# Attention of a pair of heads in three bursts, its local softmax in three whole-pair operations, and weight rounding on one engine, in a kernel of attention and two feed-forward stages

## The chip, the core and the metric

One core of a Trainium2 chip runs the whole program. It has five engines with a queue each: TensorE (matmuls, its weight loads on a row of their own), VectorE, ScalarE, GpSimd, and SyncE (SP), which here issues all transfers. An engine takes its instructions strictly in the order of its queue and waits for what they need. The metric is the device time of one execution in microseconds (us), the median of several runs; lower is better.

## What is computed

```python
# q, k, v: (4, 8, 576, 64)
q_d = q.reshape(B, H, Sd, 4, D).mean(axis=3)      # k_d, v_d likewise, Sd = 144
out_d = sm_attn(q_d, k_d, v_d)                    # coarse attention
out_up = np.repeat(out_d, 4, axis=2)
mask = np.abs(pos[:, None] - pos[None, :]) < 4    # local attention: a band of 7
out_local = softmax(where(mask, scale * q @ k.T, -1e9)) @ v
x = out_up + out_local                            # heads side by side: (4, 576, 512)
u = x + (x.T @ U @ V).T                           # U: 576x32, V: 32x576
y = u + relu(u @ w_ch1) @ w_ch2                   # 512 -> 2048 -> 512
h = relu(y @ w_in)                                # 512 -> 1024
out = (h * sigmoid(conv3(h))) @ w_out
```

Both softmaxes subtract the row's maximum and divide by the row's sum plus 1e-9.

## The kernel before

The program goes batch by batch. Everything is written out by hand in one order: lists of small functions, "slots", are run between chunks of big matmuls, and each function appends instructions to the queues of the engines it uses. No scheduler moves them afterwards.

**Stages.** In the opening (up to 69.6 us) the attention of batch 0 runs in 29 slots, with the preparation of the first 18 weight chunks and of U and V merged in (`SE`, `NS`), and `keep_warm` puts idle matmuls on TensorE. Then come four windows, `window_a(b)`: the two matmul layers of batch b over 11 of the 16 blocks of the hidden dimension (`g1_pass`, `g2_pass`; 528 big matmuls of 128x288, three for each product, since a number is held as a rounded high part and the rest, `mm3`). Between their chunks the background `bg` runs: the slots of the attention of batch b+1, and in window 0 also the other 26 chunks of weights, in windows 1 and 2 weights that are prepared and stored again (`spill`). After window 3 the five other blocks and the last two layers follow (`g12`, `g34`). I write window 0, 1, 2 for 69.6 to 187.5, 187.5 to 295.8 and 295.8 to 405.9 us.

**Attention.** A unit is a pair of heads, four pairs a batch. The queries of the local part are cut into ten windows of 64 positions (58 new ones each), six in a first group and four in a second (`LI`). The coarse part has two tiles of 72 rows for each head. So a pair has four items: coarse head 0, coarse head 1, local group 0, local group 1. Each goes through scores (matmuls into an accumulator bank), maximum, exponential, normalisation, transposition, copy of the transposed weights, and the product with the values, each step a slot or two after the one before; the items start one slot apart, the pairs five slots apart (four in the opening). The exponential is one ScalarE instruction for every 64-wide window or coarse tile, with the row's maximum as its bias and the row's sum as a second result (L390 to L392). `d_up` spreads the coarse result over four positions, `add_up` adds both into xT. Behind every second pair x is transposed (`x_step`), split into high and low part (`x_hi`, `x_lo`), multiplied with U (`x_g`), and later with V (`h_mix`).

**Banks and buffers.** There are eight accumulator banks. In the windows the big matmuls rotate over three (`psg`) and all of attention over five (`psb`). In the opening attention uses four of one pool and the three of `psg`, one bank being that of the idle matmuls.

**Weights.** A chunk of float64 weights is loaded (L169), turned into float32 words on ScalarE, VectorE and GpSimd (L125 to L142), and split: a rounded copy `dh`, then the rest on GpSimd (L152). The rounded copy is made on VectorE (L151) in the opening and in window 0, on ScalarE (L149) later.

**Transfers.** SP's queue holds, in the order written, q and k (a pair ahead), v twice (`load_vd` for the coarse, `load_vw` for the local part, the latter into tiles that the old values leave free when their last product is done), weight chunks and stores.

## Time and profile before

| | |
|---|---|
| median of three runs | 814.11 us |
| lowest | 813.95 us |
| profiled execution, its own time | 812.12 us |
| its span | 810.3 us |
| TensorE busy (matmuls) | 780.9 us, 96% |
| VectorE busy | 474.4 us, 59% |
| ScalarE busy | 416.4 us, 51% |
| GpSimd busy | 319.2 us, 39% |

The span is what the engines' rows cover; the execution's own time has a little around it. Busy shares are means over stages with different limits, so they are to be read by stretches. Starts are counted from the beginning of the span. A row of small float32 matmuls counts each twice, since it goes through the array in two passes.

### The profile page before, as it was taken

The page shows a single profiled execution, that of the slowest core. Times are in us where ns is not written, and L with a number is a line of the kernel's source. Part 1 is how long each engine was busy: PE and PEld are TensorE (multiplying, and loading weights), DVE is VectorE, ACT ScalarE, POOL GpSimd, SP SyncE. Part 2 cuts the span into 40 slices and gives each one's busy share as a digit, 9 for nine tenths or more (in the row PEclk, how much of TensorE's full clock was granted, in tenths as well). Part 3 has the DMA queues.
Part 4 walks back from the last instruction along what each step waited for, and adds up shares of the span by engine and source line. Part 5 has one row for each costly group of instructions (what it writes and reads, how often), then busy time and mean ns, then how long its engine had stood idle before and what let it go on. Part 6 is the DMA issues. An engine that isn't in the chain of part 4 may idle for free.

```text
span 810.3 us, 17088 instructions
## 1 busy us (share of the span) xinstructions
PE 780.9 (96%) x6355; PEld 719.6 (89%) x6355; DVE 474.4 (59%) x1042; ACT 416.4 (51%) x1308; POOL 319.2 (39%) x417
## 2 busy tenths in 40 slices
PE   6988997999999999999999999999999999999998
PEld 4667886899888998889999999999998999899986
DVE  6999985856766577875441213564265425752563
ACT  6996986624879769787330112432232323322332
POOL 5975674621566445764300011135123411441133
PEclk9799998999999999999999999999999999999999
DMA  7655544426476788557365262200420033002001
GB/s 203 204 145 186 171 140 148 131 88 224 115 216 208 211 270 276 169 144 217 114 251 206 99 210 97 79 1 23 133 74 1 15 128 99 0 10 69 14 1 65
DMA packets 85454, 104.37 MB, mean 129 GB/s; under 512 B 27876, under 2 KB 64124, under 8 KB 85372
## 3 DMA queue, kind: packets, MB, share of 16 engines
q1 hardware_dynamic: 85372, 103.29, 40.5%
q8 instruction: 50, 0.82, 0.4%
q14 instruction: 32, 0.26, 0.1%
HBM read 71.93 MB, written 31.33 MB: 127 GB/s over the span
## 4 chain that ended last, share of the span: by engine, by line
PE 77%; ACT 8%; DVE 5%; DMA 3%; POOL 3%; issue 2%; SPq 1%; POOLq 0%; ACTq 0%; DVEq 0%
PE psg L694 19%; PE psg L695 19%; PE psg L696 19%; PE pso L694 4%; PE pso L696 4%; PE pso L695 4%; DMA cv<-in_moe_w_ch 3%; ACT A L391 3%; ACT cq L125 2%; PE psb L448 1%; PE psb L465 1%; ACT cq L127 1%; ACT cv L126 1%; DVE cv L137 1%; PE psb L549 1%
## 5 line engine op out<-in xcount | busy, mean ns | idle before, releaser
L694 PE MATMUL psg<-h,w 128*128 128x288 f32 x352 | 108.7, 309 | 0.2 <-DVE h L721 0.2
L694 PE MATMUL psg<-uh,w 128*128 128x288 f32 x352 | 108.3, 308 | 0.5 <-ACT uh L580 0.5
L695 PE MATMUL psg<-ul,w 128*128 128x288 f32 x352 | 104.9, 298 | 0.4 <-DVE ul L585 0.4
L696 PE MATMUL psg<-uh,w 128*128 128x288 f32 x352 | 104.6, 297 | 0.0
L695 PE MATMUL psg<-h,w 128*128 128x288 f32 x352 | 104.6, 297 | 0.0
L696 PE MATMUL psg<-h,w 128*128 128x288 f32 x352 | 104.2, 296 | 0.0
L907 POOL TENSOR_TENSOR gl<-cc,gh 128x512 fp32r<-128x512 f32 x32 | 42.4, 1325 | 138.7 <-ACT gh L906 79.2
L142 POOL TENSOR_TENSOR cv<-cv,cq 128x256 int32<-128x256 int32 (+2 forms) x102 | 75.8, 743 | 12.5 <-ACT uh L580 7.5
L892 DVE SCALAR_TENSOR_TENSOR cc<-hb,cw,cc 128x576 f32<-128x576 f32 x64 | 77.2, 1206 | 1.3
L403 POOL TENSOR_TENSOR A<-A,sm 72x288 f32<-72x288 f32 (+1 forms) x64 | 46.8, 732 | 78.5 <-DVE sm L402 36.0
L125 ACT ACTIVATE cq<-cv,tiny 128x256 f16<-128x256 f32 (+2 forms) x102 | 58.8, 577 | 25.8 <-DMA cv<-in_moe_w_ch 19.9
L694 PEld LDWEIGHTS psg<-uh,w 128*128 128x128 f32 x352 | 66.7, 189 | 3.2 <-ACT uh L580 0.8
L694 PEld LDWEIGHTS psg<-h,w 128*128 128x128 f32 x352 | 66.7, 190 | 2.7 <-issue 1.1
L695 PEld LDWEIGHTS psg<-ul,w 128*128 128x128 f32 x352 | 66.6, 189 | 0.6 <-DVE ul L585 0.6
L695 PEld LDWEIGHTS psg<-h,w 128*128 128x128 f32 x352 | 67.1, 191 | 0.0
L696 PEld LDWEIGHTS psg<-h,w 128*128 128x128 f32 x352 | 66.8, 190 | 0.0
L696 PEld LDWEIGHTS psg<-uh,w 128*128 128x128 f32 x352 | 66.5, 189 | 0.0
L880 ACT ACTIVATE hb<-psg 128x288 f32<-128x288 f32 x64 | 26.2, 411 | 76.9 <-PE psg L696 76.3
L720 ACT ACTIVATE h<-psg 128x288 fp32r<-128x288 f32 x88 | 34.8, 396 | 59.7 <-PE psg L696 59.6
L132 DVE TENSOR_SCALAR cv<-cv 128x256 f32<-128x256 f32 (+2 forms) x102 | 52.0, 510 | 18.6 <-ACT cv L126 18.2
L152 POOL TENSOR_TENSOR cv<-cv 128x256 fp32r<-128x256 f32 x52 | 39.0, 750 | 59.7 <-ACT cv L149 51.9
L721 DVE SCALAR_TENSOR_TENSOR h<-psg,h 128x288 fp32r<-128x288 f32 x88 | 39.5, 450 | 29.3 <-ACT h L720 29.3
(168 smaller groups left out, 2290.3 us busy)
## 6 DMA issues: line engine op xcount, KB each, us to landing
cv<-in_moe_w_ch SPq DMA_DIRECT2D x64, 256.0 KB
ws<-cv SPq DMA_DIRECT2D x52, 256.0 KB
wb<-ws SPq DMA_DIRECT2D x15, 512.0 KB
ypb<-ys SPq DMA_DIRECT2D x40, 144.0 KB
w<-ws SPq DMA_DIRECT2D x11, 512.0 KB
qT<-in_q SPq DMA_DIRECT2D x16, 288.0 KB
kT<-in_k SPq DMA_DIRECT2D x16, 288.0 KB
vd<-in_v SPq DMA_DIRECT2D x16, 288.0 KB
```

The costliest lines, as they stand in the source:

```text
L125: nc.scalar.activation(out=q2[:, :, 1].bitcast(F16), in_=x.bitcast(F32), func=AF.Sign, bias=tiny[0:parts])
L132: nc.vector.tensor_scalar(out=xf, in0=xf, scalar1=2 * W_MIN, scalar2=2 * W_MAX, op0=ALU.max, op1=ALU.min)
L142: nc.gpsimd.tensor_tensor(out=t, in0=t, in1=qt, op=ALU.add)
L152: nc.gpsimd.tensor_tensor(out=dl, in0=tv, in1=dh.bitcast(F32), op=ALU.subtract)
L403: nc.gpsimd.tensor_tensor(out=A, in0=A, in1=sm.unsqueeze(2).to_broadcast(list(A.shape)), op=ALU.mult)
L694: nc.tensor.matmul(out=ps, lhsT=lh, rhs=rh, start=first, stop=False)
L695: nc.tensor.matmul(out=ps, lhsT=lh, rhs=rl, start=False, stop=False)
L696: nc.tensor.matmul(out=ps, lhsT=ll, rhs=rh, start=False, stop=last)
L720: after(lambda: nc.scalar.activation(out=h[:, 0, :], in_=ps, func=AF.Relu), lambda: nc.vector.scalar_tensor_tensor(out=h[:, 1, :], in0=ps, ...
L721: lambda: nc.vector.scalar_tensor_tensor(out=h[:, 1, :], in0=ps, scalar=0.0, in1=h[:, 0, :].bitcast(F32), op0=ALU.max, op1=ALU.subtract))
L892: nc.vector.scalar_tensor_tensor(out=cc, in0=hb[:, i:S + i], scalar=cw[:, i * F2 + f:i * F2 + f + 1], in1=cc, op0=ALU.mult, op1=ALU.add)
L907: nc.gpsimd.tensor_tensor(out=lo, in0=cc[:, c0:c1], in1=hi.bitcast(F32), op=ALU.subtract)
```

## The change

The four items of a pair become one unit with three bursts on TensorE: `scores` (local, then coarse, into four banks), `transposes` (coarse, then local, into three banks) and `av` (coarse, then local, into two banks). The pairs stand six slots apart in the windows (scores at slot n, transposes at n+5, values at n+7) and four in the opening (values at n+6), whose table has 27 slots. The table `FIRST` of hand-set places falls away.

The local softmax is one tile for the pair, 128 rows of ten windows of 64: one maximum (`l_max`), one subtraction on VectorE (`l_sub`), one exponential without bias and without sum (`l_exp`), one row sum on VectorE (`l_sum`), one normalisation on GpSimd. The coarse softmax keeps its four exponentials with bias and sum, and has one scaling and one normalisation a pair. The four matmuls of the coarse values alternate between the two heads. `split` makes the rounded copy on ScalarE everywhere. The transposition of x and the product with U come in three steps of up to 512 columns instead of five of 256; their sum has a bank of its own (`psum_g`), and attention rotates over four banks in the windows. `load_vw` of the next pair stands in the slot of `av`. The buffers of q and k go from three to two.

```diff
-    NS, C0, SE, W0, R0, RC = 18, 2, 29, 7, 1, 0.9
+    NS, C0, SE, W0, R0, RC = 18, 2, 27, 7, 1, 0.9
...
     def split(tv, dh, dl):
-        if hi_act[0]:
-            nc.scalar.activation(out=dh, in_=tv, func=AF.Copy)
-        else:
-            nc.vector.tensor_copy(out=dh, in_=tv)
+        nc.scalar.activation(out=dh, in_=tv, func=AF.Copy)
         nc.gpsimd.tensor_tensor(out=dl, in0=tv, in1=dh.bitcast(F32), op=ALU.subtract)
...
+        if pcount[1] and pcount[0] % 2:
+            return psg.tile([P, 512], F32, tag="g", name="psg")
+        return psb[0].tile([P, 512], F32, tag="b", name="psb", bufs=7 - PG - pcount[1])
...
-        for i in range(n):
-            nc.scalar.activation(out=A[:, i], in_=S_ap[:, i], func=AF.Exp, bias=mx[:, i:i + 1], scale=scale,
-                                 accum_out=sm[:, i:i + 1])
+    def l_sub(b, hp):
+        un = units[b, hp]
+        nc.vector.tensor_tensor(out=un.Al, in0=un.Al, in1=un.mxl.unsqueeze(2).to_broadcast([P, NT, WK]), op=ALU.add)
+    def l_exp(b, hp):
+        un = units[b, hp]
+        nc.scalar.activation(out=un.Al, in_=un.Al, func=AF.Exp)
+    def l_sum(b, hp):
+        un = units[b, hp]
+        un.sml = stat("sml", P, NT)
+        nc.vector.tensor_reduce(out=un.sml, in_=un.Al, axis=AX.X, op=ALU.add)
...
+        for kt in range(2):
+            for h in range(2):
+                nc.tensor.matmul(out=un.pso[h * D:(h + 1) * D, :], lhsT=un.vs[:, h * 2 + kt, :],
+                                 rhs=un.ATd[:, h, kt * G4:(kt + 1) * G4], start=(kt == 0), stop=(kt == 1))
...
+        V, A = (4, 6) if first else (6, 7)
...
+            put(n, 0.96 if first else 6, scores, b, hp)
+            put(n + 1, 0.3, l_mask, b, hp, 0)
+            put(n + 1, 0.4, l_mask, b, hp, 1)
+            put(n + 1, 0.6, d_max, b, hp)
+            put(n + 1, 9, d_exp, b, hp)
+            put(n + 2, 0.4, l_max, b, hp)
+            put(n + 2, 0.5, l_sub, b, hp)
+            put(n + 2, 5, l_exp, b, hp)
+            put(n + 3, 0.2, norm, b, hp, "d")
+            put(n + 3, 3, l_sum, b, hp)
+            put(n + 3, 4, norm, b, hp, "l")
+            put(n + 3, 9, v_sum, b, hp)
+            put(n + 5, 6, transposes, b, hp)
+            put(n + 5, 8, at_copy, b, hp)
+            put(n + A, 4, av, b, hp)
```

How the queue of TensorE changes, in window 1. Before, around the second pair (lines of big matmuls left out; L438 coarse transposes, L426 coarse scores, L448 coarse values, L484 local transposes, L465 local scores, L496 local values; xN is the number of matmuls in a row):

```order
L438 MATMUL psb<-ident,A 72x72 x4
L426 MATMUL psb<-kd,qd 72x144 x4
...
L448 MATMUL psb<-AT,vs 64x144 x2
L484 MATMUL psb<-ident,A 128x128 x3
...
L448 MATMUL psb<-AT,vs 64x144 x2
L484 MATMUL psb<-ident,A 128x128 x2
L465 MATMUL psb<-kT,qT 64x64 x12
...
L496 MATMUL psb<-AT,vw_142 64x61 x2
...
L465 MATMUL psb<-kT,qT 64x64 x8
```

After, around one pair (L452 coarse transposes, L456 local transposes, L433 local scores, L438 coarse scores, L478 coarse values, L486 local values):

```order
L452 MATMUL psb<-ident,Ad 72x72 x8
L456 MATMUL psb<-ident,Al 128x128 x5
...
L433 MATMUL psb<-kT,qT 64x64 x20
L438 MATMUL psb<-kd,qd 72x144 x4
...
L478 MATMUL psb<-ATd,vs 64x144 x4
L486 MATMUL psb<-ATl,vw_142 64x58 x2
L486 MATMUL psb<-ATl,vw_143 64x58 x2
```

What stood in five groups between big matmuls stands in three. Between the scores of a window's first pair and its transposes there are 60 big matmuls, between those of the other pairs at least 54 and the values of the pair before.

The queue of ScalarE in window 0, before (L125 to L127 are the start of a weight chunk, L391 the exponentials, L409 the copies of transposed weights, L454 is `d_up`):

```order
L391 ACTIVATE A,sm<-A,mx 128x64 x6
L125 ACTIVATE cq<-cv,tiny 128x256
L126 ACTIVATE cv<-cv 128x256
L127 ACTIVATE cq<-cv 128x256
...
L391 ACTIVATE A,sm<-A,mx 128x64 x4
L409 ACTIVATE AT<-psb 72x288
L125 ACTIVATE cq<-cv,tiny 128x256
L126 ACTIVATE cv<-cv 128x256
L127 ACTIVATE cq<-cv 128x256
L409 ACTIVATE AT<-psb 72x288
L391 ACTIVATE A,sm<-psb,mx 72x144 x2
```

After (L395 coarse exponentials, L494 `d_up`, L404 the local exponential, L146 the rounded copy, L465 the copies of transposed weights):

```order
L395 ACTIVATE Ad,smd<-psb,mxd 72x144 x4
L494 ACTIVATE up<-psb 128x576
L404 ACTIVATE Al<-Al 128x640
L146 ACTIVATE w<-cv 128x256
L125 ACTIVATE cq<-cv,tiny 128x256
...
L465 ACTIVATE ATd<-psb 72x288 x2
L465 ACTIVATE ATl<-psb 128x128
L465 ACTIVATE ATl<-psb 128x512
```

The ten local exponentials are one, the rounded copies have come in, and the four copies of a pair stand together behind four slots of chunk work instead of one by one between chunks.

## Rows read from the trace of the kernel before

**Rows 1.** Busy time by stretches: opening, windows 0 and 1, big matmuls alone

```profile
0.00:69.60 69.60, 55.28 (x598) 40.36 (x599) 59.73 (x159) 59.49 (x221) 52.78 (x83) 0.93 0.60 167
69.60:187.50 117.90, 110.33 (x1034) 101.21 (x1033) 85.30 (x228) 74.72 (x253) 61.61 (x80) 0.97 0.50 158
187.50:295.80 108.30, 106.90 (x1023) 98.21 (x1022) 73.70 (x194) 83.48 (x281) 54.27 (x73) 1.00 0.65 199
...
420.00:440.00 20.00, 20.00 (x153) 20.00 (x152) 2.74 (x6) 1.19 (x3) 0.00 (x0) 1.00 0.72 283
```

**Rows 2.** Waits of TensorE in the whole span: us in total, times, longest

```profile
PE psb L527 <- ACT AT L409: 5.1, 1, 5.1
...
PE psb L484 <- POOL A L403: 2.2, 1, 2.2
```

**Rows 3.** Busy time by stretches, the middle of the opening, columns as in Rows 1

```profile
40.00:60.00 20.00, 16.30 (x188) 12.22 (x189) 18.96 (x48) 19.78 (x75) 16.01 (x22) 1.00 0.51 141
```

**Rows 4.** Timeline of TensorE, window 0: start us, us, engine, line, operation

```profile
82.74 0.92 PE L465 MATMUL psb<-kT,qT 64*64 64x64 f32 x24
...
85.16 0.30 PE L696 MATMUL psg<-uh,w 128*128 128x288 f32 x1
85.38 0.68 PE L465 MATMUL psb<-kT,qT 64*64 64x64 f32 x16
...
86.23 0.29 PE L695 MATMUL psg<-ul,w 128*128 128x288 f32 x1
...
87.57 0.29 PE L696 MATMUL psg<-uh,w 128*128 128x288 f32 x1
87.70 0.43 PE L438 MATMUL psb<-ident,A 72*72 72x72 f32 x4
...
88.15 0.30 PE L695 MATMUL psg<-ul,w 128*128 128x288 f32 x1
```

**Rows 5.** Timeline of TensorE, window 1: two visits with several kinds

```profile
225.94 0.70 PE L448 MATMUL psb<-AT,vs 72*64 72x144 f32 x4
226.58 0.44 PE L484 MATMUL psb<-ident,A 128*128 128x128 f32 x2
...
229.21 0.91 PE L496 MATMUL psb<-AT,vw 128*64 128x61 f32 x24
230.05 0.68 PE L465 MATMUL psb<-kT,qT 64*64 64x64 f32 x16
230.66 0.40 PE L694 MATMUL psg<-h,w 128*128 128x288 f32 x1
```

**Rows 6.** Timeline of ScalarE, two local exponentials in a row

```profile
116.01 0.34 ACT L391 ACTIVATE A<-A,mx 128x64 f32<-128x64 f32 x1
...
116.34 0.34 ACT L391 ACTIVATE A<-A,mx 128x64 f32<-128x64 f32 x1
```

**Rows 7.** Groups by shape, whole span: busy us, mean ns of one

```profile
L896 ACT ACTIVATE cc<-cc 128x576 f32<-128x576 f32 x32 | 21.8, 681 | 17.0 <-DVE cc L892 16.9
L149 ACT ACTIVATE cv<-cv 128x256 fp32r<-128x256 f32 x52 | 21.3, 409 | 0.0
...
L151 DVE CAST w<-cv 128x256 fp32r<-128x256 f32 x44 | 21.3, 483 | 0.2
L899 DVE TENSOR_TENSOR cc<-cc,hb 128x576 f32<-128x576 f32 x32 | 24.2, 758 | 38.5 <-ACT cc L896 38.5
...
L403 POOL TENSOR_TENSOR A<-A,sm 128x384 f32<-128x384 f32 x16 | 14.6, 910 | 11.7 <-DVE sm L402 6.7 <-DVE mx L379 2.7 <-DMA vw<-in_v 1.8
```

**Rows 8.** Timelines of SP and of ScalarE around the wait in window 0

```profile
117.20 3.63 SPq L343 DMA_DIRECT2D vw<-in_v  x4
...
126.95 0.58 ACT L125 ACTIVATE cq<-cv,tiny 128x256 f16<-128x256 f32 x1 [4.64 <-DMA cv<-in_moe_w_ch]
```

**Rows 9.** Timeline of VectorE in the opening, two casts of one shape

```profile
26.08 0.99 DVE L151 CAST vh<-cv 128x192 fp32r<-128x192 f32 x1
...
29.27 0.25 DVE L151 CAST vh<-cv 128x192 fp32r<-128x192 f32 x1
```

More of the change, by code (lines that the diff above doesn't have):

```diff
@@ L287, in s5 @@
         def s5():
-            ps = psum_b()
+            ps = psg.tile([P, 512], F32, tag="g", name="psg")
             nc.tensor.transpose(out=ps[:, 0:n], in_=x["f"], identity=ident[0:n, 0:n])
@@ L306 @@
         pass
-    BUFS = {"vs": 1, "A": 4, "AT": 2}
+    BUFS = {"Al": 2}
     def tmp(b, shape, tag):
-        if b == 0:
+        if b == 0 and tag in ("vs", "Ad", "ATd"):
             return fa.tile(shape, F32, tag="h1", name=tag, bufs=HB)
-        return at.tile(shape, F32, tag=tag, name=tag, bufs=BUFS[tag])
+        return at.tile(shape, F32, tag=tag, name=tag, bufs=BUFS.get(tag, 1))
     units = {}
@@ L395, in soft_add, with stat @@
-    def soft_add(b, hp, key):
-        sm = units[b, hp].sx[key]
+        a, z = LI[i]
+        n = z - a
+        if i == 0:
+            un.Al = tmp(b, [P, NT, WK], "Al")
+        nc.vector.scalar_tensor_tensor(out=un.Al[:, a:z], in0=un.psl[i][:, 0:n * WK].rearrange("p (t c) -> p t c", t=n),
+                                       scalar=SC, in1=msk.unsqueeze(1).to_broadcast([P, n, WK]), op0=ALU.mult,
+                                       op1=ALU.add)
+    def stat(tag, parts, n):
+        return at.tile([P, n], F32, tag=tag, name=tag, bufs=2)[0:parts]
@@ new lines, in d_exp @@
+    def d_exp(b, hp):
+        un = units[b, hp]
+        un.Ad = tmp(b, [GH, 4, G4], "Ad")
+        un.smd = stat("smd", GH, 4)
+        for i in range(4):
+            nc.scalar.activation(out=un.Ad[:, i], in_=un.psd[i // 2][:, i % 2], func=AF.Exp, bias=un.mxd[:, i:i + 1],
+                                 scale=SCD, accum_out=un.smd[:, i:i + 1])
+    def l_sub(b, hp):
+        un = units[b, hp]
+        nc.vector.tensor_tensor(out=un.Al, in0=un.Al, in1=un.mxl.unsqueeze(2).to_broadcast([P, NT, WK]), op=ALU.add)
@@ L416, in keep_warm, with scores @@
             nc.tensor.matmul(out=warm[:, 0:2 * P], lhsT=one[:, 0:P], rhs=one, start=True, stop=True)
-    def d_scores(b, hp, hh):
-        if hh:
-            return
+    def scores(b, hp):
         un = units[b, hp]
+        un.psl = [psum_b(), psum_b()]
         ps = [psum_b(), psum_b()]
+        for i, (a, z) in enumerate(LI):
+            for j in range(a, z):
+                for hh in range(2):
+                    r = slice(hh * D, (hh + 1) * D)
+                    nc.tensor.matmul(out=un.psl[i][r, (j - a) * WK:(j - a + 1) * WK], lhsT=un.qT[r, WS[j]:WS[j] + WK],
+                                     rhs=un.kT[r, WS[j]:WS[j] + WK], start=True, stop=True)
         for t in range(2):
@@ new lines, in av @@
+    def av(b, hp):
+        un = units[b, hp]
+        un.psx = [psum_b(), psum_b()]
+        un.pso = un.psx[1][:, DO:DO + G4]
+        for kt in range(2):
+            for h in range(2):
+                nc.tensor.matmul(out=un.pso[h * D:(h + 1) * D, :], lhsT=un.vs[:, h * 2 + kt, :],
+                                 rhs=un.ATd[:, h, kt * G4:(kt + 1) * G4], start=(kt == 0), stop=(kt == 1))
+        AT = un.ATl.rearrange("p j (h r) -> p j h r", h=2)
+        for i in (1, 0):
+            a, z = LI[i]
+            for j in range(a, z):
+                c, n, o = Q0[j] - WS[j], Q0[j + 1] - Q0[j], Q0[j] - Q0[a]
+                for hh in range(2):
+                    nc.tensor.matmul(out=un.psx[i][hh * D:(hh + 1) * D, o:o + n], lhsT=vw[j % 2][:, j // 2, hh, :],
+                                     rhs=AT[:, j // 2, hh, c:c + n], start=True, stop=True)
@@ L451, in d_up @@
+    DO = 4 * WK
     def d_up(b, hp):
@@ L507, in x_copy @@
         ps, m, w = xs[step]
-        xf = at.tile([P, 2 * P], F32, tag="xh", name="xf", bufs=3)
+        xf = at.tile([P, 4 * P], F32, tag="xh", name="xf", bufs=2)
         nc.scalar.activation(out=xf[0:m, 0:w], in_=ps[0:m, 0:w], func=AF.Copy)
@@ L531, in x_hi @@
         ps, m, w = xs[step]
-        xh = at.tile([P, 2 * P], F32R, tag="xh", name="xh", bufs=3)
+        xh = at.tile([P, 4 * P], F32R, tag="xh", name="xh", bufs=2)
         nc.scalar.activation(out=xh[0:m, 0:w], in_=ps[0:m, 0:w], func=AF.Copy)
@@ L537, in x_lo @@
         ps, m, w, xh = xs[step]
-        xl = at.tile([P, 2 * P], F32R, tag="xl", name="xl", bufs=2)
+        xl = at.tile([P, 4 * P], F32R, tag="xl", name="xl", bufs=1)
         nc.vector.tensor_tensor(out=xl[0:m, 0:w], in0=ps[0:m, 0:w], in1=xh[0:m, 0:w].bitcast(F32), op=ALU.subtract)
```

214 lines of the change are left out of this document (70 added, 144 removed).

## The prediction

> **What bounds the kernel now.** I read the stages first. [rows 1] are five stretches (columns: length, then busy time and instructions of TensorE's matmuls, its weight loads, VectorE, ScalarE, GpSimd, then granted clock, DMA share, GB/s). TensorE is busy 55.28 us of the first 69.60 us, the opening, in which batch 0's attention and the first weights are prepared, and 106.90 of 108.30 us in window 1, so from 69.6 us on the kernel lasts as long as TensorE's own queue plus its waits. The last row is a stretch of big matmuls alone: 153 in 20.00 us, 0.131 us each. Window 0 (69.60 to 187.50 us) does the same TensorE work as window 1 and lasts 9.6 us longer, at a mean clock of 0.97. The waits of TensorE [rows 2] name one large one there, 5.1 us. In the opening TensorE is not the bound: in a middle stretch [rows 3] ScalarE is busy 19.78 of 20.00 us, VectorE 18.96, GpSimd 16.01. So there are three places to look: what small matmuls cost between big ones, ScalarE in the opening, and the one wait.
>
> **What a visit costs.** Call a group of small matmuls between two big ones a visit. In [rows 4] the big matmul at 85.16 us is the last before a visit of 16 passes (8 matmuls in two passes each), and the second big one after it starts at 86.23: 1.07 us, less two big ones (0.26), is 0.81. The visit of 24 passes spans 0.92 us against 0.68: eight passes are 0.24 us, 0.03 each. So of 0.81 us 0.48 is passes, and 0.33 is there however little is in the visit: some 0.16 to go in and as much to come out. The transposes (L438, four passes, 87.57 to 88.15 us) cost 0.32 in all; their pass is 0.07, so only 0.04 is fixed. In [rows 5] 24 passes of L496 and then 16 of L465 take 1.45 us to the next big matmul. At 0.03 each the passes are 1.2, so the change of kind costs some of the 0.25 left: 0.14 to 0.17 again. I price every such switch at 0.16 us.
>
> Before, the order shows a pair of heads in five visits, and I count the switches (transposes and big matmuls need none between them): transposes with coarse scores 2, coarse values with local transposes 2 (twice, the second time with local scores behind: 4 instead), local values with local scores 3, local values with transposes 2: 13 a pair. After, scores have 3 (in, local to coarse, out), transposes 0, values 2: 5. Coarse behind local transposes, and coarse before local values, stand side by side in no row; if each pair were a change of kind, it would be 7. I take 5, since in each the two kinds fill as many output columns of the array (all for the transposes, 64 a head for the values), while local and coarse scores do not (64 and 72). Eight fewer are 1.28 us a pair, six 0.96.
>
> The Trainium skill, page "TensorEngine Tiling (Array Packing)", section Key Properties, says that changing the tiling mode, not just the tile, drains TensorE. By that rule the gain over twelve pairs is 15.4 us of switches, by the count of seven 11.5. The trace agrees as far as it goes: transposes beside big matmuls, both of the full array, cost next to nothing extra [rows 4].
>
> The coarse values' four matmuls are also reordered: two heads now alternate, as the local ones do. Before, four passes of 144 columns take 0.64 us with one switch [rows 5], 0.12 each or 0.83 ns a column; the alternating passes of [rows 4] have 64 columns in 0.03 us, 0.47 ns a column, so two run side by side. No trace row has coarse values alternating. If they pair, eight passes cost 0.5 instead of 1.0 us. Bounds 0 and 0.5; I take 0.5, since the local ones, as wide in output, do it. Together 1.78 us a pair, 12 pairs in windows 0 to 2: 21.3 us. The x transposes and their products in three larger steps instead of five lie mostly in no-switch company: 0 to 1.4 us a window, I take 0.5: 1.5 us. **Visits: -22.8 us**, bounds -12 (twelve pairs at 0.96) and -26.
>
> **The opening.** Ten local exponentials start 0.33 us apart [rows 6], 3.3 us a pair; the one over 128x640 is bounded by the 128x64 row (0.34) and by the 128x576 sigmoid's 0.681 scaled, 0.76 [rows 7]. I take 0.73, less the 0.1 by which neighbours overlap: 2.7 us less a pair, 10.8 in four. Against it stand the roundings that come over from VectorE: 18 chunks and 7 setup pieces, 0.41 each as L149 [rows 7], 0.3 after overlap: 7 us. ScalarE gets 3.8 us shorter. VectorE loses 25 casts of 0.48 (12 us, L151) and four small additions and reciprocals a pair, and gains a subtraction and a row sum a pair, each like L899 (758 ns for 576 columns, 0.84 for 640): 6.7 us. GpSimd multiplies the same elements. So ScalarE stays the bound and sets the pace. The table has 27 slots instead of 29. **Opening: -4 us**, bounds 0 (VectorE or GpSimd takes over at once) and -7 (two slots of 69.6/29 = 2.4 us each, and the first pair sooner).
>
> **The wait in window 0.** SP issued the local values' loads from 117.20 us, once TensorE had finished with the old ones, and the next weight chunk behind them; ScalarE then stood 4.64 us at that chunk's first instruction [rows 8], with the copies of transposed weights behind it, for which TensorE waited. In the order after, those loads stand in the slot of the values, and the next copies four slots later, where before they stood in the next slot. Between them the order now has 42 to 54 big matmuls, 5.5 to 7.1 us, plus visits: that covers the stand. The 9.6 us hold the wait and the slower clock behind it. **-6 us**, bounds 0 and -9.6.
>
> **What it adds.** From scores to transposes the chain is now mask, maxima, subtraction, exponential, sum, normalisation: three VectorE passes of 0.84, 0.73 on ScalarE, a GpSimd multiplication of 1.5 (L403's 910 ns for 384 columns, scaled), and some 2 us for masks, coarse maxima and small ones: 6.8 us if nothing stands ahead. The order puts 60 big matmuls (7.9 us) there for the first pair of a window, for others at least 54 and a value burst of 2 us: 9.1. Other work in the queues can make the first pair up to 1 us late, and the last x product now stands one slot ahead of its mix. I add **+3 us** for three windows, bounds 0 and +18 (below).
>
> Costed at nothing: ScalarE rounds 26 chunks more in window 0 (8 us, against 10.8 saved; it is busy 74.72 of 117.90 us; without cover 8 us); two instead of three buffers for q and k (loaded a pair ahead still); the extra accumulator bank.
>
> **Sum.** 22.8 + 4 + 6 - 3 = 29.8 us off. The profiled execution took 812.12 us, its span 810.3; so 782.3. The median of the runs, 814.11, lies 2.0 above that execution: 784. Of this kernel a measurement can tell about 2% from no change: faster means under 797.8, slower over 830.4.
>
> **Rivals.**
> *The chain comes late.* If each of 12 bursts of transposes waits for one more GpSimd multiplication, 1.5 us, 18 us come back: 802. For it: the chain is longer by three operations in series. Against it: TensorE waited for GpSimd's A 2.2 us at the longest [rows 2], and GpSimd is busy only 54.27 of 108.30 us. 0.13.
> *It does less than it says.* The coarse values don't pair (6 us) and window 0's wait stays (6): 796. For it: the loads still stand ahead of a weight chunk on SP. 0.12.
> *The subtraction holds GpSimd up.* A VectorE cast took 0.99 us beside a busy GpSimd and 0.25 otherwise [rows 9]. The subtraction, with both operands in SBUF, may be held for as long as a multiplication, 1.4 us, where its chain is tight: four pairs in the opening, three first pairs: 9.8 us, 794. 0.05. The Trainium skill, page "SBUF — State Buffer", section Who interferes with whom, says that a VectorE instruction with two SBUF inputs contends with GpSimd reads; it speaks against moving the maximum from ScalarE's bias into a VectorE operation. No row here shows a subtraction beside GpSimd; the cast's two times agree with such a hold.
> *Slower: the banks.* The scores now take four accumulator banks at once, all of their pool, and three of those are the transposes', freed by the last of four ScalarE copies one slot ahead. If ScalarE stands before these copies as in [rows 8], a burst waits some 4 us: 12 x 4 = 48, 832. The gain is gone at 2.5 us a burst and 2% are lost at 3.9. Against it: ScalarE is busy 83.48 of 108.30 us in window 1 and gets some 11 us lighter. 0.05.
> *All of it.* No new wait, 7 in the opening, 9.6 in window 0: 774. 0.05.
>
> **How the numbers follow.** My forecast has 0.60, and 784 is its time. 770 to 800 holds it and all cases but the late chain and the banks, 0.82. Faster: 0.60 + 0.12 + 0.05 + 0.05 = 0.82; same: 0.13; slower: 0.05.
>
> **What would show it.** After: a pair's visits 5.3 us in all, eight passes of coarse values near 0.5 us; windows 1 and 2 near 100 us; the opening near 66 us; no wait over 2 us of TensorE in window 0; ScalarE's local exponential near 0.73 us. Waits of transposes for GpSimd's Al, or of scores for ScalarE's copies, summing to over 10 us would make it wrong, as would an opening longer than 69.6 us.

## The result: 820.9 us, no faster than before

The changed kernel takes 820.91 us (820.08 to 822.12), beside it the kernel before 814.17: ratio 1.0085, interval 1.0065 to 1.0105: slower by 0.9%, clear of noise. The predicted 784 (770 to 800) is missed by 37 us, with the wrong sign. The profiled execution took 822.12 us, its span 820.3. Busy time by stretches of the changed kernel (columns as in [rows 1]; opening, its middle, windows 0, 1, 2):

```profile
0.00:81.50 81.50, 55.97 (x599) 45.61 (x600) 58.41 (x120) 56.42 (x168) 48.96 (x75) 0.80 0.52 146
40.00:60.00 20.00, 13.31 (x149) 11.17 (x146) 15.27 (x32) 13.82 (x42) 11.39 (x14) 0.74 0.44 128
81.50:198.60 117.10, 108.55 (x1033) 103.76 (x1033) 84.13 (x179) 72.64 (x201) 58.04 (x72) 0.94 0.50 158
198.60:304.20 105.60, 99.56 (x1023) 95.72 (x1022) 80.52 (x174) 72.31 (x201) 54.02 (x65) 1.00 0.65 199
304.20:416.10 111.90, 102.32 (x1022) 97.39 (x1021) 83.04 (x170) 70.70 (x198) 59.80 (x72) 0.98 0.60 188
```

Against [rows 1]: the opening grew from 69.6 to 81.5 us, and no engine fills its middle any more (ScalarE 13.82 of 20, where [rows 3] had 19.78). Windows 0 to 2 last 334.6 us in all, before 336.3. TensorE's busy time in them fell by 14.7 us (325.1 to 310.4), its idle time rose from 11.2 to 24.2. So two things are to be explained: 12 us in the opening, 13 us of new waits. A third, smaller one is the clock: 14.7 us is less than the 22.8 forecast, and most of what is missing is in window 0, where the same TensorE work kept it busy for 108.55 us at a mean granted clock of 0.94, and in window 1 for 99.56 at 1.00. TensorE's waits in windows 0 to 2 of the changed kernel (us in total, times, longest):

```profile
PE psg L680 <- DVE h L707: 9.0, 8, 2.5
PE psb L438 <- DVE kd L356: 6.6, 4, 2.2
PE psb L456 <- DVE xl L537: 3.2, 2, 2.3
PE psb L478 <- DVE Al L371: 2.6, 2, 1.3
...
PE psb L456 <- POOL Al L416: 0.6, 2, 0.4
```

All the large ones are for VectorE: big matmuls for the pass that makes the low part of h and so frees a bank (L707), coarse scores for the sums of q and k (`kd`), local transposes for a bank that the low part of x is still read from (`xl`, L537), values for a bank that the masks read (L371). Transposes hardly wait for GpSimd's Al.

All runs in one table: median in us, then opening and windows 0 to 2 together in the profiled execution, and how much of the windows TensorE stood idle. What follows them takes 404 to 406 us in every run. Six runs have the changed kernel's opening unaltered; theirs took 81.3 to 84.3 us. Three have its windows unaltered (after, e1, f5); theirs took 334.1 to 338.4, with 23.7 to 25.2 idle. So a difference of 2 us in an opening, or of 4 in the windows, says little in one profile; the idle time is steadier, since it leaves out what a lower granted clock adds to the busy time.

| run | median | opening | windows 0-2 | idle in them |
|---|---|---|---|---|
| before | 814.2 | 69.6 | 336.3 | 11.2 |
| after | 820.9 | 81.5 | 334.6 | 24.2 |
| e1_open_vectore | 818.1 | 76.7 | 338.4 | 23.7 |
| e2_before_scalare | 817.3 | 73.7 | 334.4 | 8.7 |
| e3_all_vectore | 815.1 | 75.1 | 333.3 | 24.8 |
| e4_vsum_later | 826.1 | 83.6 | 335.3 | 26.9 |
| f5_copies_later | 818.5 | 78.4 | 334.1 | 25.2 |
| f6_sums_earlier | 828.1 | 82.0 | 340.8 | 27.2 |
| f7_no_norm | 807.4 | 84.3 | 321.2 | 15.3 |
| f8_softmax_scalare | 857.4 | 81.9 | 371.6 | 46.1 |
| g1_two_inputs | 832.8 | 81.8 | 341.7 | 31.4 |
| g3_before_two_inputs | 817.2 | 74.4 | 336.8 | 13.2 |
| h1_vectore_copies_later | 815.9 | 74.2 | 331.0 | 23.8 |
| h2_sums_in_quiet_slot | 815.9 | 81.3 | 327.4 | 18.0 |
| m0_both_orders | 805.9 | 75.0 | 325.8 | 18.6 |
| m1_norm_vectore | 817.5 | 73.9 | 335.8 | 24.8 |
| m2_vsum_opening | 808.6 | 76.0 | 323.9 | 18.3 |
| p1_values_by_head | 822.1 | 82.3 | 338.3 | 27.8 |
| x1_open_no_norm | 803.2 | 72.8 | 324.3 | 18.6 |
| z1_chain_spread | 824.8 | 73.6 | 344.0 | 29.3 |

### The profile page after: what moved, and what is told of

The parts are those of the page before. It is cut to its first block, busy times and chain, and to the rows that moved or that the text cites. A ratio compares the mean times of both kernels' runs of the same rounds, so it can differ in the third digit from the quotient of the medians.

```text
span 820.3 us, 16557 instructions
## 1 busy us (share of the span) xinstructions
PE 767.0 (93%) x6355; PEld 722.9 (88%) x6355; DVE 486.2 (59%) x915; ACT 389.2 (47%) x1043; POOL 312.4 (38%) x385
## 4 chain that ended last, share of the span: by engine, by line
PE 68%; DVE 8%; ACT 7%; DMA 6%; POOL 4%; issue 4%; SPq 2%; DVEq 0%; POOLq 0%; ACTq 0%
PE psg L680 17%; PE psg L681 16%; PE psg L682 16%; PE pso L680 4%; PE pso L682 4%; PE pso L681 4%; DVE cv L132 2%; DMA cv<-in_moe_w_ch 2%; ACT Ad L395 1%; ACT cq L125 1%; DMA cv<-in_moe_w_out 1%; PE psb L486 1%; DMA us<-ul 1%; DVE cv L137 1%; ACT cv L126 1%
## 5 line engine op out<-in xcount | busy, mean ns | idle before, releaser
L680 PE MATMUL psg<-uh,w 128*128 128x288 f32 x352 | 109.3, 311 | 9.2 <-DVE h L707 8.7
L682 PE MATMUL psg<-uh,w 128*128 128x288 f32 x352 | 105.8, 301 | 0.0
L137 DVE TENSOR_SCALAR cv<-cv 128x256 int32<-128x256 int32 (+2 forms) x102 | 69.2, 678 | 29.5 <-POOL w L147 16.9
L680 PEld LDWEIGHTS psg<-uh,w 128*128 128x128 f32 x352 | 67.9, 193 | 13.0 <-DVE h L707 11.1
L147 POOL TENSOR_TENSOR cv<-cv 128x256 fp32r<-128x256 f32 x52 | 40.7, 783 | 79.8 <-ACT cv L146 58.0
L125 ACT ACTIVATE cq<-cv,tiny 128x256 f16<-128x256 f32 (+2 forms) x102 | 58.8, 577 | 23.7 <-DMA cv<-in_moe_w_ch 13.9
L682 PEld LDWEIGHTS psg<-uh,w 128*128 128x128 f32 x352 | 67.6, 192 | 0.0
L132 DVE TENSOR_SCALAR cv<-cv 128x256 f32<-128x256 f32 (+2 forms) x102 | 60.0, 588 | 12.1 <-ACT cv L126 12.0
L866 ACT ACTIVATE hb<-psg 128x288 f32<-128x288 f32 x64 | 26.2, 411 | 76.7 <-PE psg L682 76.1
L707 DVE SCALAR_TENSOR_TENSOR h<-psg,h 128x288 fp32r<-128x288 f32 x88 | 39.1, 449 | 23.5 <-ACT h L706 23.2
```

What stands on the lines that cost most here:

```text
L125: nc.scalar.activation(out=q2[:, :, 1].bitcast(F16), in_=x.bitcast(F32), func=AF.Sign, bias=tiny[0:parts])
L132: nc.vector.tensor_scalar(out=xf, in0=xf, scalar1=2 * W_MIN, scalar2=2 * W_MAX, op0=ALU.max, op1=ALU.min)
L137: nc.vector.tensor_scalar(out=t, in0=x[0], scalar1=3, scalar2=None, op0=ALU.logical_shift_left)
L147: nc.gpsimd.tensor_tensor(out=dl, in0=tv, in1=dh.bitcast(F32), op=ALU.subtract)
L680: nc.tensor.matmul(out=ps, lhsT=lh, rhs=rh, start=first, stop=False)
L682: nc.tensor.matmul(out=ps, lhsT=ll, rhs=rh, start=False, stop=last)
```

## Experiments on the opening

What stands still there, first. Waits of ScalarE, GpSimd and VectorE in the opening of the changed kernel:

```profile
ACT ATd L465 <- PE psg L452: 6.0, 3, 3.0
...
ACT ATd L465 <- PE psb L452: 2.6, 1, 2.6
...
POOL w L147 <- ACT w L146: 14.6, 8, 6.3
POOL vl L147 <- ACT vh L146: 7.4, 2, 6.0
...
DVE cv L137 <- POOL w L147: 8.7, 7, 3.6
```

Read it as a ring. The shift L137 needs a t buffer, which GpSimd's remainder L147 frees; L147 needs ScalarE's rounded copy L146; that stands in ScalarE's queue behind the pair's copies L465, which wait for the transposes; and the transposes wait for a bank that the next masks free, which stand behind L137. Once round, at 50 to 59 us (pieces of the timelines of VectorE, TensorE, ScalarE, GpSimd and VectorE again):

```profile
50.41 0.55 DVE L371 SCALAR_TENSOR_TENSOR Al<-psb,msk 128x384 f32<-128x384 f32 x1
...
51.43 0.68 PE L452 MATMUL psg<-ident,Ad 72*72 72x72 f32 x4 [2.89 <-DVE Al L371]
...
52.62 0.41 ACT L465 ACTIVATE ATd<-psb 72x288 f32<-72x288 f32 x1 [2.56 <-PE psb L452]
...
56.87 0.43 ACT L146 ACTIVATE w<-cv 128x256 fp32r<-128x256 f32 x1
...
57.38 0.73 POOL L147 TENSOR_TENSOR w<-cv,w 128x256 fp32r<-128x256 f32 x1 [6.31 <-ACT w L146]
...
58.14 0.81 DVE L137 TENSOR_SCALAR cv<-cv 128x256 int32<-128x256 int32 x1 [3.58 <-POOL w L147]
```

The ring is a reading of these waits; what undoing each link is worth, the next runs show.

**Is it the rounding or the bursts?** A square of four kernels: the rounding put back in the changed kernel (in the opening alone, and in window 0 too), and the rounding alone moved in the kernel before (shortened).

```
 # e1: after; e3: the same with hi_act[0] = b > 0
-        nc.scalar.activation(out=dh, in_=tv, func=AF.Copy)
+        if hi_act[0]: nc.scalar.activation(out=dh, in_=tv, func=AF.Copy)
+        else: nc.vector.tensor_copy(out=dh, in_=tv)
+            hi_act[0] = True          # at the head of window b
 # e2: before
-    hi_act = [False]
+    hi_act = [True]
```

> The changed kernel with one part undone: in the opening alone (batch 0's attention ahead of window 0) the rounded copy of a weight chunk is VectorE's again, as before; from window 0 on it is ScalarE's. Theory R (rounding closes a loop over four engines: VectorE's shift waits for a t buffer, that for GpSimd's remainder, that for the rounded copy in ScalarE's queue behind the pair's copies and exponentials): the opening falls from 81.5 us to 66-70, the kernel from 820.9 to 806-810 us. Rival B (the bursts alone lengthen the opening, by a chain of one pair that is longer than its four slots): the opening stays at 79-83 us, the kernel at 818-823.

> The changed kernel with the rounded copies on VectorE in the opening and in window 0, as before the change: the bursts and the softmax alone. Beside the run with the opening alone it prices window 0. Theory V (in the windows TensorE now waits for a VectorE that comes late): 26 casts of 0.3-0.5 us more on VectorE make window 0 some 2-6 us longer than its 117.1. Rival S (ScalarE's queue held window 0 up): window 0 gets 2-5 us shorter. The opening by theory R 66-70 us, by rival B 79-83.

> The kernel before with one part of the change alone: every rounded copy of a weight chunk on ScalarE, in the opening and in window 0 too. Theory R (rounding closes the loop): the opening grows from 69.6 us to 76-82, the kernel from 814 to 820-827 us. Rival B (the bursts alone): ScalarE was busy 19.78 of 20.00 us there, so the opening grows by the seven us of roundings at the most and rather by 0-3 us, the kernel is at 813-818 us.

The opening goes 69.6, with the rounding moved alone 73.7, with the rest of the change alone 75.1 or 76.7, with both 81.5. Neither theory has it all: the two add up, the rounding being worth 4 to 6 us and the rest 5 to 8. In the kernel before with the rounding on ScalarE its middle reads:

```profile
40.00:60.00 20.00, 16.49 (x211) 12.52 (x210) 16.48 (x39) 19.84 (x83) 14.12 (x19) 1.00 0.47 136
```

There ScalarE was full and stayed full: with the old order ScalarE is busy 6.3 us longer in the opening (65.75 for 59.49), and the opening takes 4.1 us more. In the changed kernel ScalarE is not full, and the same roundings cost at least as much.

Two things beside the ring change with the rounding, and no run separates them from it. VectorE's shift and clamp of the weight chunks take 22.4 us in the opening before, 28.0 in e2 and 29.3 in the changed kernel, but 24.3 in e3: with the rounding on ScalarE they are held longer beside GpSimd (how, the next section shows), and the masks stand behind them. And TensorE's granted clock in the middle of the opening is 1.00 before and in e2, 0.83 in e3, 0.74 in the changed kernel; the four transposes at 51.43 above, at the lower of the clock's two levels, take 0.68 us where [rows 4] had 0.43 at the higher. Window 0 is 115.4 us with the rounding on VectorE (e3) and 117.1 on ScalarE: neither theory of window 0 shows beyond the spread.

**The place of the copies.** Before, the copies of local weights stood one slot behind their transposes, those of the coarse ones in the same slot; the change puts all four into the slot of the transposes, so ScalarE meets them while TensorE has not begun. Here they stand a slot later:

```
-            put(n + 5, 8, at_copy, b, hp)
+            put(n + 6 if first else n + 5, 2 if first else 8, at_copy, b, hp)
```

> The changed kernel with one edit in the opening alone: a pair's four ScalarE copies of transposed weights stand one slot later (ahead of the values), where they stood before the change, and not in the slot of the transposes. Theory C (ScalarE stands 12 us in front of these copies waiting for TensorE, and the roundings are queued behind them, for which GpSimd stands 22 us and then VectorE's shift 12): the opening falls from 81.5 to 72-76 us, the kernel to 812-816. Rival L (the opening is as long as one pair's chain, and a slot more in it makes it longer): the opening stays at 81.5 or gets up to 3 us longer.

> The changed kernel with both edits of the opening: rounded copies on VectorE in the opening and window 0, and the copies of transposed weights one slot later in the opening. Theory A (two separate causes: 6.4 us by the rounding, 3.1 by the place of the copies): the opening is at 71-73 us, the kernel at 809-813. Rival O (both break the same loop, whichever is undone): the opening stays at 75-77, the kernel at 813-817.

Alone it brings the opening from 81.5 to 78.4 us, 3.1 us where theory C gave 5.5 to 9.5. ScalarE then waits elsewhere, and GpSimd still for the rounding (waits of both in that opening):

```profile
ACT Ad L395 <- DVE mxd L383: 9.0, 4, 3.2
...
POOL w L147 <- ACT w L146: 11.0, 7, 3.1
```

On top of the rounding it gives 1 to 2 us: 75.1 and 76.7 (e3, e1) without it, 73.6 to 75.0 in the four runs that have both (h1, m0, m1, z1), and the median of h1 is no better than that of e3. The two edits do not add up: mostly the same ring, cut at another place, as rival O had it.

**What is left.** Two more runs on the combined kernel described below: GpSimd's additions for the coarse values a slot earlier (`put(n + 2, 9, v_sum, b, hp)` in the opening too), and the opening without its normalisations.

> The same as the first of these runs, and GpSimd's additions for the coarse values (1.3 and 0.8 us) stand one slot earlier in the opening too, ahead of the normalisations. In the chain of the opening they stand between the local normalisation and the addition of the next weight chunk, for which VectorE's clamp and behind it the next pair's masks wait. Theory L (what is left of the opening, 74 against 69.6 us, is that chain, about 2 us in each of the first pairs): the opening falls to 70-72 us. Rival: it stays within 1 us, since VectorE, busy 18 of 20 us there, is the bound.

> The combined kernel without GpSimd's two multiplications by the reciprocal sums in the opening (batch 0's attention weights stay unnormalised). VectorE is busy 18 of 20 us in the middle of the opening, a third of it in clamp and shift that are held. Theory G (these holds are what is left of the opening's loss, 75 against 69.6 us): it falls to 69-72 us. Rival D (the loop of masks, transposes, copies and banks of one pair sets the pace): 74-76 us.

76.0 and 72.8, against 73.6 to 75.0 us of the four runs with both edits. The additions are not it. Without GpSimd's two multiplications shift and clamp take 18.8 us in the opening, against 25.2 in m0, but the opening gets only 1 to 2 us shorter, at the edge of the spread: so the holds by these multiplications are a small part of it. Some 4 to 5 us of the 12 stay open in the combined kernel.

## Experiments on the windows

**Why is VectorE late?** It has three passes of 0.8 us a pair for the local softmax, where before it had two maxima. And its passes over weight chunks are held: a shift in the opening while GpSimd stands still, then one in window 2, and what GpSimd did meanwhile (changed kernel):

```profile
52.48 0.28 DVE L137 TENSOR_SCALAR cv<-cv 128x256 int32<-128x256 int32 x1
...
341.88 2.87 DVE L137 TENSOR_SCALAR cv<-cv 128x256 int32<-128x256 int32 x1 [1.38 <-POOL cv L147]
...
341.81 0.73 POOL L142 TENSOR_TENSOR cv<-cv,cq 128x256 int32<-128x256 int32 x1
342.50 0.73 POOL L147 TENSOR_TENSOR cv<-cv 128x256 fp32r<-128x256 f32 x1
343.19 0.72 POOL L142 TENSOR_TENSOR cv<-cv,cq 128x256 int32<-128x256 int32 x1
343.87 0.73 POOL L147 TENSOR_TENSOR cv<-cv 128x256 fp32r<-128x256 f32 x1
344.83 0.73 POOL L142 TENSOR_TENSOR cv<-cv,cq 128x256 int32<-128x256 int32 x1 [0.23 <-DVE cv L137]
```

A pass that takes 0.28 us alone lasts 2.87, over four operations of GpSimd in a row, until these break off at 344.60; the next one needs the result of this very shift. Not every hold lasts until such a break: of 33 shifts and clamps that took over 0.9 us, 25 ended just after one of GpSimd's additions for the coarse values had begun, while its row went on. And not every pass is held: the row sum (L409) took 0.78 to 0.82 us in all sixteen of its runs, though in ten of them GpSimd was at work when it began. Shift and clamp in windows 0 to 2 (busy, mean ns of one), of the changed kernel:

```profile
L137 DVE TENSOR_SCALAR cv<-cv 128x256 int32<-128x256 int32 (+1 forms) x79 | 53.7, 680 | 17.5 <-POOL w L147 8.2 <-POOL cv L147 4.1
L132 DVE TENSOR_SCALAR cv<-cv 128x256 f32<-128x256 f32 (+1 forms) x79 | 46.2, 584 | 7.7 <-ACT cv L126 7.6
```

and of the kernel before:

```profile
L132 DVE TENSOR_SCALAR cv<-cv 128x256 f32<-128x256 f32 (+1 forms) x79 | 40.0, 507 | 15.1 <-ACT cv L126 14.9
L137 DVE TENSOR_SCALAR cv<-cv 128x256 int32<-128x256 int32 (+1 forms) x79 | 38.2, 483 | 5.4
```

22 us more for the same 79 chunks. The Trainium skill, page "SBUF — State Buffer", section Who interferes with whom, says that copies, casts and passes with constants can take the port pair that VectorE shares with GpSimd, and that whoever comes first has it for the whole instruction, the other being blocked. These rows agree that the pass that comes second is held, here over four instructions and not one. My prediction weighed only that section's rule on two inputs.

Could another form of the passes escape? The second input is a constant column spread over the row, for the clamp likewise; in the changed kernel and in the one before.

```
-        nc.vector.tensor_scalar(out=t, in0=x[0], scalar1=3, scalar2=None, op0=ALU.logical_shift_left)
+        nc.vector.tensor_tensor(out=t, in0=x[0], in1=three[0:parts].to_broadcast([parts, n]), op=ALU.logical_shift_left)
```

> The changed kernel with VectorE's clamp and shift of a weight chunk in a form with two inputs (the second a constant, spread over the row) in place of the form with one input and constants; the same values. Theory G (it is GpSimd's running operations that hold these one-input passes, 0.28 us alone, up to 2.9 us, while the two-input subtraction took 0.83 us in nearly every one of its runs): no pass is over 0.7 us, their sum in windows 0 to 2 falls from 100 us to 65 or less, the waits of TensorE for h, kd and Al (18 us) fall by half, windows 0 to 2 get 8-15 us shorter in all and the opening 3-7, the kernel 800-811. Rival P (any pass with SBUF inputs is held alike, or GpSimd is slowed instead): the sum stays over 85 us, or GpSimd's operations get longer by as much, and the kernel stays at 817-825.

> The kernel before with the same edit alone (clamp and shift with two inputs). The holds there were some 11 us in the opening and about as much a window, but TensorE waited little for VectorE. Theory G, with VectorE's lateness as a thing of the new order: the passes get as flat as in the run beside it, the kernel gains 0-5 us (810-815). Rival: VectorE's holds cost the kernel before as much as the changed one, then it gains 10 us or more (below 806).

Theory G was wrong on the form. The rows of the changed kernel with it, windows 0 to 2:

```profile
L142 DVE TENSOR_TENSOR cv<-cv,three 128x256 int32<-128x256 int32 (+1 forms) x79 | 59.1, 748 | 17.5 <-POOL w L152 8.3 <-POOL cv L152 4.0
L136 DVE SCALAR_TENSOR_TENSOR cv<-cv,wmax 128x256 f32<-128x256 f32 (+1 forms) x79 | 58.9, 745 | 2.7 <-ACT cv L130 2.5
```

Two-input passes are held as well, and the kernel took 832.8 us; the kernel before took 2.5 us more by the same edit. By the Trainium skill's rule on two inputs (same page and section) that was to be expected; the trace agrees. Part of the loss is the form's own time: with GpSimd still, such a pass takes 0.42 us instead of 0.28, so the holds alone come to about the same in both forms, 0.33 and 0.35 us a pass (estimates from these means). In the changed kernel's windows the subtraction took 0.83 us in eleven of its twelve runs, since GpSimd stood still when it began, and 1.35 us in the twelfth, when GpSimd was at work.

**Holds or own work?** Without the normalisations in the windows (f7, on the changed kernel), and with the local one on VectorE (m1, on the combined kernel m0 described below); shortened:

```
 # f7
-        nc.gpsimd.tensor_tensor(out=A, ...)
+        if b == 0:
+            nc.gpsimd.tensor_tensor(out=A, ...)
 # m1
-        nc.gpsimd.tensor_tensor(out=A, ...)
+        eng = nc.vector if b and key == "l" else nc.gpsimd
+        eng.tensor_tensor(out=A, ...)
```

> The changed kernel without GpSimd's two multiplications by the reciprocal sums in windows 0 to 2 (the attention weights of batches 1 to 3 stay unnormalised). It takes away 2.4 us of GpSimd a pair, and with it the longest stretches in which VectorE's shift and clamp (0.28 us alone) are held, up to 2.9 us. Theory G (the holds make VectorE late): shift and clamp take some 8 us less a window, the waits for h, kd and Al (18 us) fall by half or more, windows 0 to 2 get 8-15 us shorter in all, the kernel 806-813. Rival V (VectorE is late by its own three long passes a pair): holds shrink, but windows by less than 4 us.

> The same as the run beside it, and the local weights of the windows are normalised by VectorE (0.83 us, as the subtraction of this size) in place of GpSimd (1.26 us). Theory G (VectorE loses more by holds under GpSimd's long operations than by its own work): the sums of clamp and shift fall by 3 us a window or more, windows 0 to 2 get 3-8 us shorter than in the run beside it. Rival V (VectorE's own work makes it late): the windows get 3-8 us longer, with more waits for the low parts of h.

Without them windows 0 to 2 are 13.4 us shorter (8.5, 4.6 and 0.3), 8.9 of it idle time of TensorE, and clamp and shift take 20 us less (99.9 to 79.9). This run leaves out GpSimd's work as well as the holds, and the chain of a pair gets shorter by it. With the local one on VectorE clamp and shift fall too, from 85.9 to 75.4 us, yet the windows get 10 us longer, 6.2 of it idle time, and TensorE waits more for h, first in m0, then in m1 (the line numbers move with the edits):

```profile
PE psg L685 <- DVE h L712: 10.4, 7, 2.8
```

```profile
PE psg L686 <- DVE h L713: 15.7, 7, 3.8
```

So VectorE's own passes make it late, and f7 agrees with the holds doing so too; a pass of 0.83 us more a pair in VectorE's queue outweighs the holds that it saves. How the 13 us divide between the two is not settled.

**The queue's order.** The sums of q and k three slots ahead of the scores, or two; with the latter GpSimd's additions a slot earlier; and these additions two slots later (e4, in the opening too).

```
-            put(n - 1, 7.06 if first else 3, qk_sum, b, hp)
+            put(n - 1 if first else max(n - 3, 0), 7.06 if first else 3, qk_sum, b, hp)   # f6; h2: n - 2
-            put(n + 3, 9, v_sum, b, hp)
+            put(n + 3 if first else n + 2, 9, v_sum, b, hp)                               # h2; e4: n + 5
```

> The changed kernel with the sums of q and k two slots earlier in the windows (three slots ahead of the scores). Theory V (VectorE is late by its own work and by holds, and each thing that stands close behind it makes TensorE wait): the waits of coarse scores for kd in windows 0 to 2, 6.6 us, fall under 2, and the three windows get 3-6 us shorter, the kernel 815-818. Rival M (the lateness is only moved: what stands behind the sums in VectorE's queue is then late): windows within 2 us of before, the waits for h grow by as much.

> The changed kernel with, in the windows, the sums of q and k one slot earlier (two ahead of the scores, in a slot in which the pair before has nothing on VectorE; three ahead they had stood before that pair's row sum, and the kernel took 7 us more) and GpSimd's two additions one slot earlier, ahead of the normalisations. Theory Q (what matters is what stands ahead of the chain in VectorE's and GpSimd's queues): the waits for kd (6.6 us) fall under 2 and those for Al stay under 4, windows 0 to 2 get 4-8 us shorter in all, the kernel 813-817. Rival (lateness is only passed on to the low parts of h): within 2 us of 820.9.

> The changed kernel with GpSimd's two additions for the coarse values (1.3 and 0.7 us) two slots later, so that they no longer stand right behind the two normalisations (1.1 and 1.2 us). Theory G (VectorE's shift and clamp of a weight chunk take 0.28 us alone, but up to 2.9 us while GpSimd runs one long operation after another; behind them stand the sums of q and k and the low parts for which TensorE waits, 18 us in all): windows 0 to 2 get 3-8 us shorter together, the waits of coarse scores for kd and of big matmuls for h fall by half. Rival (VectorE is late by its own three longer passes a pair): within 2 us of the changed kernel, waits as they were.

Three ahead, the waits for kd vanish, and yet the windows take 6 us more and the median rises by 7. TensorE's waits there:

```profile
PE psg L680 <- DVE h L707: 10.6, 6, 2.9
PE psb L478 <- DVE Al L371: 5.5, 4, 1.9
PE psb L456 <- POOL Al L416: 4.0, 4, 1.2
```

The sums (1.5 us) now stood ahead of the pair before's row sum, so its normalisation came late: waits for Al rose from 0.6 to 4.0 us. Two ahead, in a slot where that pair has nothing on VectorE, the windows take 7.2 us less, 6.2 of it idle time, as theory Q said. The waits for kd, 6.6 us, are gone; what the additions' place gave is not separated from it. The additions later: 0.7 us more in the windows and 5 us more in the median, against theory G.

**The softmax itself.** In the windows exponentials with bias and sum again, no subtraction and no row sum.

```
+            for i in range(NT):
+                nc.scalar.activation(out=un.Al[:, i], in_=un.Al[:, i], func=AF.Exp, bias=un.mxl[:, i:i + 1], scale=1.0,
+                                     accum_out=un.sml[:, i:i + 1])
```

> The changed kernel with the local softmax of windows 0 to 2 as before: ten exponentials with bias and accumulated sums on ScalarE, no subtraction and no row sum on VectorE. VectorE gets 1.6 us lighter a pair, ScalarE some 2.7 us heavier. Theory V (its own longer passes make VectorE late): the waits for h, kd and Al (18 us) fall by half, windows 0 to 2 get 5-9 us shorter in all, the kernel 812-816. Rival G (holds by GpSimd make it late): the waits stay within a third of what they were, the kernel 818-823.

Neither theory: 37 us more, 22 of it idle time of TensorE and 15 busy time, at a granted clock of 0.92 for 0.97. The ten exponentials stand in a row, VectorE stands in front of their sums with the low parts of h behind it, and TensorE waits for these (waits of VectorE, then of TensorE):

```profile
DVE sml L420 <- ACT Al L407: 24.4, 11, 2.6
...
PE psg L688 <- DVE h L715: 19.8, 6, 5.3
```

So in this order of slots the three whole-pair operations are what makes the bursts bearable, though they load VectorE.

**The values' heads in turn.** `for kt: for h:` against `for h: for kt:` as before.

> The changed kernel with the coarse values' four matmuls head by head, as before the change, in place of the heads in turn. It sizes one term of the sum: 0.5 us a pair, 6 us in twelve pairs. Theory (two heads in turn run side by side): the values' visits grow from 2.0 to 2.5 us, TensorE's busy time by some 6 us, and the kernel takes 2-6 us more where TensorE does not wait anyway. Rival (they did not pair): visits and busy time stay within 0.1 us a pair.

A values' visit of the changed kernel, then of this run (timelines of TensorE):

```profile
239.01 0.29 PE L682 MATMUL psg<-h,w 128*128 128x288 f32 x1
239.24 0.71 PE L478 MATMUL psb<-ATd,vs 72*64 72x144 f32 x8
239.78 1.33 PE L486 MATMUL psb<-ATl,vw 128*64 128x58 f32 x40
241.04 0.40 PE L680 MATMUL psg<-h,w 128*128 128x288 f32 x1
```

```profile
238.44 0.72 PE L478 MATMUL psb<-ATd,vs 72*64 72x144 f32 x8
238.98 1.34 PE L486 MATMUL psb<-ATl,vw 128*64 128x58 f32 x40
```

Eight coarse passes take 0.54 us either way, and TensorE's busy time in the windows is the same (310.5 and 310.4 us): the order of the heads is worth nothing.

**Together.** m0 is the changed kernel with the edits of e3, f5 and h2; z1 spreads its chain over one slot more.

> The changed kernel with the edits of the opening (rounded copies on VectorE in the opening and window 0, copies of transposed weights a slot later in the opening) and those of the windows (sums of q and k two slots ahead of the scores, GpSimd's additions for the coarse values ahead of the normalisations). Theory A (the opening and the windows lose for separate reasons): opening 73-75 us, windows 0 to 2 near 326-329 in all, the kernel 804-809. Rival O (TensorE's waits for VectorE come back, since VectorE is fuller by the casts in window 0): windows 333 or more, the kernel 811-816.

> The combined kernel (805.9 us: both edits of the opening, both of the windows) with the local softmax of the windows spread over one slot more: the subtraction and the exponential one slot later, so that the maxima and the subtraction (1.6 us together) no longer stand in one slot, the row sum and the local normalisation another, transposes and values one later too. Theory V (TensorE waits for the low parts of h, 10.4 us, since a slot's passes of VectorE stand between two of them): these waits fall to 6 us or less, windows 0 to 2 get 3-7 us shorter in all, the kernel 799-803. Rival (they are as long as the held clamp and shift of a chunk, which stay): within 2 us of 805.9, or above it as the last pair of a window ends a slot later.

m0 takes 805.88 us, ratio to the kernel before 0.9876 (0.9827 to 0.9925): faster than both, theory A, and against the kernel before by 1.2%, clear of noise but less than 2%. Opening 75.0, windows 107.6, 103.1 and 115.1. Against the changed kernel 6.4 us of window 0's gain are busy time, at a granted clock of 1.00 for 0.94, and window 2 loses 3.2 us, at 0.94 for 0.98. z1 was a mistake of mine that teaches: one slot later the transposes share a slot with the next pair's scores, seven banks of the four that attention rotates over, and a wait for the copies is there (waits of TensorE):

```profile
PE psg L686 <- DVE h L713: 15.1, 8, 3.2
PE psb L461 <- POOL Al L421: 6.0, 4, 2.1
PE psb L438 <- ACT ATd L470: 2.7, 2, 2.1
```

The last row is the prediction's rival of the banks in kind, brought about by one slot. In size it is the smaller part: against m0 the waits for h rose by 4.7 us and those for Al by 3.7.

## Why the prediction was wrong

The forecast of the profiled execution was 782.3 us and it took 822.1, 40 more. By terms: the opening missed by 16 us, TensorE's waits by 16 (forecast -6 and +3, measured +13), the visits by 8.

**Visits (-22.8, measured -14.7): the size of a pair right by luck.** A pair's undisturbed visits take 2.15 (scores), 1.09 (transposes) and 2.00 us, 5.24 in all, 5.3 predicted; before, an undisturbed pair in window 1 took 7.02, so 1.78 less, as forecast. But two errors cancel in it. The 0.5 us for heads in turn is no such thing (p1): the slow row in [rows 5] carried the change to the transposes behind it. And 1.78 us over the eight switches saved would be 0.22 each, not 0.16 (an estimate). TensorE's busy time fell by 7.3 us in window 1, as four pairs at 1.78 would have it, in window 2 by 5.5, in window 0 by 1.8 only, at a granted clock of 0.94 instead of 0.97. The sum had no term for a clock lower than before.

**Opening (-4): the step that failed worst, 11.9 us the other way.** "So ScalarE stays the bound and sets the pace" was worked out from busy sums. ScalarE did get lighter, 59.5 to 56.4 us, and its local exponential takes 0.734 us (0.73 predicted). But it stopped being the bound: it stood in front of copies that now follow their transposes in the same slot, with the roundings behind. I had listed the roundings by price and never asked who waits for one (GpSimd's remainder, then the t buffer) and what stands ahead of it. Moving the rounding back is worth 5 to 6 us of the opening (e1, e3); that it costs by this ring, and not by the longer holds or the lower clock that come with it, is a reading. VectorE, forecast to lose 12 us of casts and to gain 6.7, got only 1.3 us lighter (59.73 to 58.41), since shift and clamp took 6.9 us more.

**Wait in window 0 (-6): gone as forecast, and eaten.** No wait of over 2.3 us is left there, and none for a transfer; its idle time is 8.5 us all the same, where before it was 7.6, nearly all of it for VectorE.

**What it adds (+3): the other step that failed.** I looked for the new waits where a burst needs its own chain or a bank. Both came out as forecast: 0.6 us for Al, no copies. What I did not cost is VectorE in the windows at all: three passes of 0.8 us a pair in one queue with the low parts of h and the sums of q and k. TensorE waited 21 us for what that queue does (h, kd, xl and the masks' Al). The rival on GpSimd's holds had the mechanism and, for the most part, the wrong victim: clamp and shift (22 us more), not the subtraction (0.869 us on average, held in one run of twelve). My bound of +18 would have covered it, but as bound of another cause.

**Signs.** An opening over 69.6 us was named as the sign against it, and came; windows 1 and 2 took 106 and 112 us, not near 100; the waits for Al and for copies, the other sign, did not come.

## What to carry to other kernels

An operation that moves to a lighter engine takes its place in that engine's queue: look at what stands ahead of it and at who waits for it, before adding busy times. When TensorE gets faster work, the next wait is with the engine that frees its banks; cost that engine's queue in the same stretch, even at 70% busy. A table of slots can be worth more than the change: here a few entries and the engine of the rounding made 820.9 into 805.9 us. And read waits apart from busy time, since busy time moves with the granted clock too: with the same windows TensorE was busy 310 us in the changed kernel and 315 in e1.

## What was not expected of the hardware

A 128x256 shift or clamp of VectorE over SBUF lasts up to 2.87 us beside GpSimd instead of 0.28, held over four of GpSimd's operations in a row, in the form with constants (584 and 680 ns on average) as in the form with two inputs (745 and 748, of which 0.42 us is the pass alone). A row sum of 128x640 is not held: 0.78 to 0.82 us with GpSimd at work or still. Coarse values with two heads in turn go no faster than head by head, 0.54 us for eight passes.
